# One unit of weights, two batches' products and the copies of own rows assigned to other tiles in the first chunk of a fused mixer and two MLPs

## The chip, the cores and the metric

One core of one Trainium2 chip runs the whole program in a single launch. The metric is device time in microseconds (us), lower is better. Engine names as in the profile: PE is TensorE, PEld its weight loads, DVE is VectorE, ACT is ScalarE, POOL is GpSimd, SP is the queue from which nearly all DMAs are issued.

## The reference, cut to what matters

A state-space mixer over 4 batches of 768 positions, in chunks, then two MLPs on its 3072 tokens of width 256 (hidden width 2048, softplus in the first, a sigmoid gelu in the second):

```python
for c in range(nc):
    cum = np.cumsum(la, axis=-1)
    L = np.exp(cum[:, :, :, None] - cum[:, :, None, :]) * causal
    M = np.einsum('bhin,bhjn->bhij', Cc, Bc) * L
    y_intra = np.einsum('bhij,bhjd->bhid', M, xc)
    y_inter = np.einsum('bhin,bhnd->bhid', Cc, state) * np.exp(cum)[..., None]
    y[:, :, sl] = y_intra + y_inter
    Bx = np.einsum('bhjn,bhjd->bhjnd', Bc, xc) * decay_from_j[:, :, :, None, None]
    state = decay_full[:, :, None, None] * state + np.sum(Bx, axis=2)
...
h = x @ w_in
g = softplus(h)
x = g @ w_out
```

## The kernel before, in words

**Tokens.** The kernel cuts the 768 positions into 6 chunks of 128. A chunk of all four batches is 512 tokens wide. A "batch" number s below counts (chunk, batch) pairs: s = 0 to 3 are chunk 0, s = 4 to 7 chunk 1, and so on up to 23. The mixer of s = 0 to 3 is done ahead of everything; the mixer of s = 4 and up runs spread over the tiles of the first MLP, one chunk ahead of it.

**Tiles.** The first MLP is a loop over t (line 912): 6 chunks of 16 tiles, a tile being 128 of the 2048 hidden columns. `g1` (line 439) makes the tile's hidden values with six matmuls, because both operands are split into a high part that the fast matmul format holds exactly and a low rest (wh·xh, wh·xl, wl·xh for two halves of the contraction). `hidden` is the softplus on ACT. `g2` (line 457) multiplies the tile's activations into the two output accumulators, two tiles later: `g2(t - 2, ...)` is issued at tile t. For the tiles of the first chunk below 10 (`PLAIN`) it is a plain f32 matmul per accumulator on weights `w1of`; from tile 10 on it is three matmuls per accumulator, of which the first reads `w1ol`, the low rest of the output weights, then `w1oh` twice, with `gh` and `gl` (the activation and its rest; `rnd` on ACT, `low` on DVE, a subtraction at line 85).

**Weights.** They arrive as 64-bit words and are put together during the first chunk, in units of 256 columns or rows: `W1_units` lists them, 13 in all, alternately input ("1i") and output ("1o"), and the unit at place u of the list is called unit u here. `unit(t)` (line 895) joins unit t: for an output unit two DVE instructions (lines 148 and 153), for an input unit one (line 161). Where the unit is split, `split` (line 93) puts the copy to the high part (ACT, line 95) and the subtraction that makes the low rest (DVE, line 85, writing `w1il` or `w1ol`) on two lists, which `catch_up` empties in the next tiles. `w_low` does the ACT part of the joining, `w_scale` a scaling on POOL (input, line 130) or ACT (output, line 128). The last units are 9, 11 and 12: the output rows of tiles 10 and 11, 12 and 13, 14 and 15.

**The mixer's steps for one s**, dealt to tiles by hand (k = t mod 4, s = (c + 1)*4 + (t mod 16)//4): `at_scan` (DVE, line 260) makes L; `at_m` (DVE, line 339) multiplies it with the kept product CB, in place, once per half g, giving M; `at_y` and `at_u` (PE, lines 367, 376, 385) make y and the state's increment u for a pair of batches; `at_out` copies y to `xh` on ACT (line 404) and hands back the subtraction for `xl` (DVE, line 85); `at_state` updates the state (DVE, line 419) and calls `at_own` (POOL, line 426), the copy of the state's own rows, which the next `at_y` of that batch reads; `at_small` is `at_bs` (POOL, line 273, reads L, so that `at_m`, which overwrites L, comes behind it) and `at_dc` (DVE line 283, then POOL line 285, giving `cd`). `at_prep` makes masked operands (DVE line 228 twice, then three subtractions on POOL at line 88, writing `lb` and `rhs_bd`) for s = 8 and up. `at_load_a` and `at_load_p` issue DMAs on SP.

**Order.** Everything runs under a manual schedule: each engine, and the SP queue, takes its instructions in the order of the program text. An instruction that waits holds up all that is behind it on its engine. Within a tile of the loop the order is: `at_m`; `w_low`; `low(t - 1)`; `g1`; `g2`; `at_y`/`at_u`; the ACT copies of `at_out`; `hidden`; `rnd`; `catch_up` of the DVE list, then of the ACT list; then by k the block with `xl`, `at_scan`, `at_state`, `at_small`, `at_prep`, the loads; then `unit(t)`.

Before the change, batches 4 and 5 have M at tiles 0, 2, 6 and 7, y and u at tile 7, and `xh`, `xl`, state and `at_small(6)` at tile 8; M of batch 6 is at tiles 9 and 10; the four first `at_own` are at tile 2; unit 12 is joined at tile 12 and its low rest made at tile 14. At tile 15 DVE has `low(14)`, `xl` of batches 6 and 7, the scan of batch 8, the states of 6 and 7.

Of the kernel before, what the change touches and what calls it, by code (L numbers as in the profile page):

```python
# [19 lines left out]
NB, NH, S, D, N = 4, 8, 768, 32, 16  # L20
# [5 lines left out]
NF = DFF // P  # L26
# [17 lines left out]
def mixer_two_mlps(ctx: ExitStack, tc: tile.TileContext, pack_p, pack_q, pack_s, pack_x, a_rows, consts, w1i, w1o, w2i, w2o, out):  # L44
# [46 lines left out]
    act_later, vec_later = [], []  # L91
# [8 lines left out]
    def catch_up(todo):  # L100
        fs = todo[:]
        todo.clear()
        for f in fs:
            f()
# [76 lines left out]
    def at_load(s):  # L181
        at_load_a(s)
        at_load_p(s)
# [14 lines left out]
    def at_load_p(s):  # L198
        c, b = divmod(s, NB)
        d = sub.setdefault(s, {})  # L200
        if c == 0:
            pk = x2[:, (0, 1, 4, 5)[s]].rearrange("p k t -> p (k t)")
            nc.sync.dma_start(out=pk[:, 0:PL_W], in_=pack_p[s])
            d["B"], d["C"], d["x"], d["bn"] = pk[:, 0:PL_C], pk[:, PL_C:PL_X], pk[:, PL_X:PL_BN], pk[:, PL_BN:PL_W]
        else:
            px = at.tile([P, SX_W], F32, tag="px", name=f"px{s}", bufs=3)
            nc.sync.dma_start(out=px, in_=pack_x[s - NB])
            if c > 1:
                pk = at.tile([P, SP_W], F32, tag="pk", name=f"pk{s}")
                nc.sync.dma_start(out=pk, in_=pack_s[s - 2 * NB])  # L210
                d["B"], d["C"] = pk[:, 0:SP_C], pk[:, SP_C:SP_W]
            d["x"], d["bn"], d["ci"] = px[:, 0:SX_BN], px[:, SX_BN:SX_CI], px[:, SX_CI:SX_W]
# [52 lines left out]
    def at_small(s):  # L265
        at_bs(s)
        at_dc(s)
# [60 lines left out]
    def at_m(s, g):  # L328
        d = sub[s]
        l = d["L"][:, 4 * g : 4 * g + 4, :]  # L330
        if s >= NB:
            d["M", g] = l
        elif s == 0:
            d["M", g] = d["cb", g].rearrange("p a t -> p (a t)").rearrange("p (h t) -> p h t", h=4)
        else:
            m = hid.tile([P, TB], F32, tag=("gh", "g", "gh")[s - 1], name=f"M{s}_{g}")
            d["M", g] = m.rearrange("p (h t) -> p h t", h=4)
        m, l = (v.rearrange("p (a h) t -> p a (h t)", a=2) for v in (d["M", g], l))
        (nc.gpsimd if s == 0 else nc.vector).tensor_tensor(out=m, in0=d["cb", g], in1=l, op=ALU.mult)  # L339
# [67 lines left out]
    def at_state(s):  # L407
        c, b = divmod(s, NB)
        d = sub.pop(s)
        if c == NC - 1:  # L410
            return
        u = d["u"]
        st = state[b]
        if s < 2:
            nc.scalar.activation(st, u, AF.Copy)
        elif c == 0:
            nc.vector.tensor_copy(st, u)
        else:
            nc.vector.scalar_tensor_tensor(
                out=st, in0=st, scalar=d["dc"][:, T - 1 : T], in1=u, op0=ALU.mult, op1=ALU.add  # L420
            )
        if c > 0:
            at_own(b)
# [4 lines left out]
    def at_pe(s, k):  # L428
        if k < 2:
            at_cb(s, k)  # L430
        elif k == 2 and s % 2:
            at_y(s - 1, s)
            at_u(s - 1)
            at_u(s)
# [66 lines left out]
    with tc.manual_schedule():  # L501
# [140 lines left out]
        W1_units = []  # L642
        for q in range(6):
            W1_units += [("1i", q + 2), ("1o", q + 1)]
        W1_units += [("1o", 7)]
        SLOT = {7: 0, 8: 1}
        W2_units = [(kind, q) for q in range(8) for kind in ("2i", "2o")]
        W_in = {"1i": w1i, "1o": w1o, "2i": w2i, "2o": w2o}

        def w_low(kind, q):  # L650
            (w_three_sign if kind == "1i" else w_three)(kind, q)
# [243 lines left out]
        def unit(t):  # L895
            nonlocal wt
            kind, q = W1_units[t]
            if kind == "1o":
                w_join_lo(wt, raws[kind, q].bitcast(U32)[:, 0::2])
            if kind == "1o" and 2 * q >= PLAIN:  # L900
                wo_split((w1oh, w1ol), q, w_join_sign(kind, q, wt))
            elif kind == "1o":
                w_join_sign(kind, q, wt, w1of[:, 2 * q : 2 * q + 2, :].rearrange("p m f -> p (m f)"))
            else:
                wi_split(W1, q, w_join(kind, q, wt))
            if t + 1 < len(W1_units):
                wt = w_scale(*W1_units[t + 1], nc.gpsimd if W1_units[t + 1][0] == "1i" else nc.scalar)
            for u in {9: (12,)}.get(t, (t + 5,) if t < 7 else ()):
                kind, q = W1_units[u]
                w_load(W_in[kind], kind, q, SLOT.get(u))  # L910

        for t in range(NT):
            c, m = divmod(t, NF)
            s, k = (c + 1) * NB + m // 4, m % 4
            mixing = c < NC - 1
            ended = (t - 2) // NF if t >= 2 and (t - 2) % NF == NF - 1 else None

            m_at = (2, 3) if s == NB + 1 else (1, 2)
            if mixing and k in m_at and t > 1:
                at_m(s, m_at.index(k))  # L920
            if 1 < t < len(W1_units):
                w_low(*W1_units[t])
            if t > PLAIN:
                low(t - 1)

            if t != 1:
                g1(t, *W1, xh[c], xl[c])
            late = k < 2 or t < NF
            if mixing and not late:
                at_pe(s, k)  # L930
            if t >= 2:
                for j in range(2):
                    g2(t - 2, j)
            if mixing and late:
                at_pe(s, {(NB + 1, 2): 3, (NB + 1, 3): 2}.get((s, k), k))

            pair_done = () if not mixing else (s - 1, s) if k == 3 and s % 2 and s > NB + 1 else (NB, NB + 1) if t == 2 * 4 else ()
            xl_of = [at_out(i) for i in pair_done]
            if t != 1:
                hidden(t)  # L940
            if t >= PLAIN:
                rnd(t)
            if ended is not None:
                finish(ended, 0)
                finish(ended, 1)
            if t == 0:
                g1(1, *W1, xh[c], xl[c])
                hidden(1)
                w_low(*W1_units[0])
                unit(0)  # L950
                at_bs(s)
                at_m(s, 0)
                catch_up(act_later)
                w_low(*W1_units[1])
            catch_up(vec_later)
            catch_up(act_later)

            if t == 2:
                for i in range(NB):
                    at_own(i)  # L960
            if mixing:
                if k == 0 and t > 0:
                    for f in xl_of:
                        f()
                    for i in pair_done:
                        at_state(i)
                    at_small(s)
                elif k == 1:
                    if 2 * NB <= s + 1 < NSUB:
                        at_prep(s + 1)  # L970
                elif k == 3:
                    for f in xl_of:
                        f()
                    if s + 1 < NSUB:
                        at_scan(s + 1)
                    for i in pair_done:
                        at_state(i)
                    if s + 2 < NSUB:
                        at_load(s + 2)
                    if s == NSUB - 1:  # L980
                        at_ctx.close()
                        y_ctx.close()
                        ps_y = ps_ctx.enter_context(tc.tile_pool(name="ps_y2", bufs=2, space=PSUM, reuse_waits="tile"))

            if t == PLAIN - 1:
                w1oh, w1ol = (wts.tile([P, NF, DM], F32R, tag=n, name=n) for n in ("w1oh", "w1ol"))
            if 0 < t < len(W1_units):
                unit(t)
            if t == 1:
                at_dc(s)  # L990
            if NF - 2 <= t < NF - 2 + PLAIN and m % 2 == 0:
                q = (t - NF + 2) // 2
                wo_split((w1oh, w1ol), q, w1of[:, 2 * q : 2 * q + 2, :])
            if t == (NC - 2) * NF:
                for kind, q in W2_units[0:3]:
                    w_load(W_in[kind], kind, q)
                units = [unit_steps(0), unit_steps(1)]
                first, then, srcs = pair_sums(0)
                pair = [first + then]
            if t == (NC - 1) * NF:  # L1000
                second_open()
                pair[0] += pair_split(0, [], srcs)
                units += [unit_steps(u) for u in range(2, 9)]
            if t >= (NC - 1) * NF - 3:
                run(units, pair, "DADAD", True)
# [59 lines left out]
```

## Time and profile before

| | us |
|---|---|
| Median of 3 runs (lowest, highest) | 568.26 (568.26, 568.55) |
| The profiled execution: its own time | 568.49 |
| The profiled execution: span, first to last instruction | 566.7 |
| Busy in the span: PE | 558.0 (98%) |
| Busy in the span: DVE | 441.1 (78%) |
| Busy in the span: ACT | 341.0 (60%) |
| Busy in the span: POOL | 134.2 (24%) |

How to read it: the span is the time between the first and the last instruction; the run's own time is 1.8 us more, for what lies around it. Busy shares are averages over the whole span; what a change of one stage does is read from the timeline of that stage. In the timeline a line has the start, the busy time (of a merged group from its first start to its last end), engine, line, operation, tile names, shapes, a count, and, in brackets, how long the engine had been idle before and what ended that. Matmuls overlap: six of 0.39 us follow one another 0.23 us apart. The first tile's matmuls begin at 21.17 us; tile 7 begins at 39.16, tile 10 at 50.82, tile 14 at 62.91, tile 16 at 71.44.

### The profile page before, as it was taken

Reading aid. Unit: us, or ns where it says so; the run is one execution under the profiler, and the core shown is the slowest. Engines: PE = TensorE matmul, PEld = TensorE weight load, DVE = VectorE, ACT = ScalarE, POOL = GpSimd, SP = SyncE. Lnnn points to the kernel's source line nnn. Section 1 sums busy time; section 2 is a strip of 40 time slices with the busy share of each in tenths; the row PEclk is TensorE's granted clock in tenths of the full one; section 3 lists DMA queues with packets and bytes.
Section 4 is the critical chain, followed back from the end, with each engine's and each line's share of the span. In section 5 each row is a group of like instructions: output and inputs, shape, how many; then the busy total and the mean of one; then the engine's idle time right before and its main releaser. Section 6 shows DMA issues by size and latency. Waiting matters only on the chain.

```text
span 566.7 us, 8296 instructions
## 1 busy us (share of the span) xinstructions
PE 558.0 (98%) x3092; PEld 450.2 (79%) x3092; DVE 441.1 (78%) x645; ACT 341.0 (60%) x574; POOL 134.2 (24%) x128
## 2 busy tenths in 40 slices
PE   8999999999999999999999999999999999999997
PEld 6656788888888888888888788888888888888885
DVE  7999999869787776968888699998976565665754
ACT  4989555444344444435898777867755464654644
POOL 4684474546544544541000000000000000000000
PEclk9999999999999999999999999999999999999999
DMA  8965443341422425211233112000200000200002
GB/s 285 376 195 174 160 134 106 133 154 42 154 90 106 133 104 205 103 56 34 80 110 107 44 41 72 1 1 0 75 1 1 1 1 0 75 0 1 1 1 74
DMA packets 22745, 48.64 MB, mean 86 GB/s; under 512 B 1936, under 2 KB 5168, under 8 KB 22704
## 3 DMA queue, kind: packets, MB, share of 16 engines
q1 hardware_dynamic: 22560, 48.01, 25.5%
q8 instruction: 24, 0.39, 0.3%
q14 instruction: 17, 0.14, 0.1%
q10 hardware_dynamic: 144, 0.10, 0.1%
HBM read 44.76 MB, written 3.34 MB: 85 GB/s over the span
## 4 chain that ended last, share of the span: by engine, by line
PE 86%; DMA 4%; DVE 4%; POOL 2%; ACT 2%; issue 1%; SPq 0%; POOLq 0%; DVEq 0%
PE h L447 20%; PE p L838 19%; PE o L812 8%; PE o L814 8%; PE o L813 8%; PE o L466 7%; PE o L467 6%; PE o L468 6%; DMA wraw_1i<-w1i 2%; PE y L376 2%; DMA px<-pack_x 2%; PE cb L322 1%; PE y L367 1%; POOL so L426 1%; DVE L L260 1%
## 5 line engine op out<-in xcount | busy, mean ns | idle before, releaser
L85 DVE TENSOR_TENSOR gl<-g,gh 128x512 fp32r<-128x512 f32 x182 | 141.1, 777 | 24.4 <-ACT gh L478 23.7
L473 ACT ACTIVATE g<-h 128x512 f32<-128x512 f32 x96 | 57.5, 599 | 107.5 <-PE h L447 95.4
L478 ACT ACTIVATE gh<-g 128x512 fp32r<-128x512 f32 x182 | 115.1, 632 | 5.9
L447 PE MATMUL h<-xh,w1ih 128*128 128x512 f32 x192 | 78.7, 411 | 0.0
L447 PE MATMUL h<-xl,w1ih 128*128 128x512 f32 x192 | 75.1, 392 | 0.0
L844 DVE TENSOR_TENSOR g<-p,x 128x512 f32<-128x512 f32 x72 | 49.6, 689 | 29.6 <-PE p L838 28.2
L466 PE MATMUL o<-gh,w1ol 128*128 128x512 f32 x172 | 68.0, 395 | 0.7 <-DVE w1ol L85 0.7
L467 PE MATMUL o<-gh,w1oh 128*128 128x512 f32 x172 | 67.0, 390 | 0.0
L468 PE MATMUL o<-gl,w1oh 128*128 128x512 f32 x172 | 67.0, 389 | 0.0
L260 DVE TENSOR_TENSOR_SCAN L<-abz,eye 128x1024 f32<-128x1024 f32 (+1 forms) x26 | 63.2, 2439 | 0.7 <-PE abz L250 0.7
L447 PE MATMUL h<-xh,w1il 128*128 128x512 f32 x192 | 59.3, 390 | 0.0
L846 ACT ACTIVATE g<-g 128x512 f32<-128x512 f32 x72 | 45.5, 632 | 20.9 <-DVE g L844 18.5
L88 POOL TENSOR_TENSOR rhs_bd<-tc,pk 64x512 fp32r<-64x512 f32 x32 | 54.8, 1714 | 1.2
L812 PE MATMUL o<-gh,w2ol 128*128 128x512 f32 x120 | 46.8, 390 | 0.4 <-ACT gh L478 0.4
L814 PE MATMUL o<-gl,w2oh 128*128 128x512 f32 x120 | 46.9, 390 | 0.0
L813 PE MATMUL o<-gh,w2oh 128*128 128x512 f32 x120 | 46.7, 389 | 0.0
L846 ACT ACTIVATE g<-p 128x512 f32<-128x512 f32 x24 | 14.3, 594 | 52.4 <-PE p L838 52.3
L447 PEld LDWEIGHTS h<-xh,w1ih 128*128 128x128 f32 x192 | 36.0, 188 | 8.6 <-issue 1.9
L447 PEld LDWEIGHTS h<-xl,w1ih 128*128 128x128 f32 x192 | 36.1, 188 | 8.3 <-issue 2.2
L447 PEld LDWEIGHTS h<-xh,w1il 128*128 128x128 f32 x192 | 36.0, 188 | 7.9
L466 PEld LDWEIGHTS o<-gh,w1ol 128*128 128x128 f32 x172 | 32.3, 188 | 8.6 <-DVE w1ol L85 1.1
L339 DVE TENSOR_TENSOR L<-cb,L 128x512 f32<-128x512 f32 x32 | 21.9, 685 | 20.8 <-PE cb L322 20.4
(193 smaller groups left out, 1057.2 us busy)
## 6 DMA issues: line engine op xcount, KB each, us to landing
abz<-scr_z SPq DMA_DIRECT2D x20, 512.0 KB, 7.1
pk<-pack_s SPq DMA_DIRECT2D x16, 512.0 KB, 4.2
px<-pack_x SPq DMA_DIRECT2D x20, 256.0 KB, 3.4
wraw_2i<-w2i SPq DMA_DIRECT2D x8, 512.0 KB, 4.9
wraw_2o<-w2o SPq DMA_DIRECT2D x8, 512.0 KB, 3.6
out<-ot SPq DMA_DIRECT2D x11, 256.0 KB, 2.0
wraw_1i<-w1i SPq DMA_DIRECT2D x5, 512.0 KB, 5.8
wraw_1o<-w1o SPq DMA_DIRECT2D x5, 512.0 KB, 5.1
```

The costliest lines, as they stand in the source:

```text
L85: nc.vector.tensor_sub(o, x, y)
L260: nc.vector.tensor_tensor_scan(out=d["L"][:, h].rearrange("p h t -> p (h t)"), data0=ab.rearrange("p h t -> p (h t)"), data1=eye8[:, h].re ...
L447: nc.tensor.matmul(h, w[:, k, f], x[:, k, :], start=(n == 0), stop=(n == 5))
L466: nc.tensor.matmul(a, w1ol[:, m, o], d["gh"], start=first, stop=False)
L467: nc.tensor.matmul(a, w1oh[:, m, o], d["gh"], start=False, stop=False)
L468: nc.tensor.matmul(a, w1oh[:, m, o], d["gl"], start=False, stop=last)
L478: nc.scalar.activation(d["gh"], d["g"], AF.Copy)
L812: nc.tensor.matmul(a, wl, d["gh"], start=first, stop=False)
L813: nc.tensor.matmul(a, wh, d["gh"], start=False, stop=False)
L814: nc.tensor.matmul(a, wh, d["gl"], start=False, stop=last)
L838: nc.tensor.matmul(dst, w, x, start=start and i == 0, stop=i == 2, skip_group_check=not start)
L846: nc.scalar.activation(d["g"], src, AF.Gelu_apprx_sigmoid)
```

## The change

It concerns tiles 2 to 15, the first chunk of the first MLP. No instruction is added or taken away; they are placed at other tiles.

- M of batch 5 moves from tiles 6 and 7 to 8 and 9, M of batch 6 from 9 and 10 to 11 and 12 (table `M_AT`); M of batch 7 stays at 13 and 14.
- y and u of batches 4 and 5 move from tile 7 to tile 9; what follows them (`xh`, `xl`, state, `at_small(6)`) moves from tile 8 to tile 10, and the DMA of batch 7's inputs (`at_load_p(7)`) from tile 7 to tile 10.
- The four `at_own` on POOL move from tile 2 to tile 6.
- Unit 12 is joined at the end of tile 14 instead of tile 12, and a new emptying of the DVE list at the very end of tile 15, behind the scan of batch 8 and the states, issues its low rest and that of the first re-split output unit (which stood in tile 16).

```diff
@@ -644,6 +644,7 @@
         SLOT = {7: 0, 8: 1}
+        M_AT = {2: ((4, 1),), 8: ((5, 0),), 9: ((5, 1),), 11: ((6, 0),), 12: ((6, 1),), 13: ((7, 0),), 14: ((7, 1),)}
...
-            m_at = (2, 3) if s == NB + 1 else (1, 2)
-            if mixing and k in m_at and t > 1:
-                at_m(s, m_at.index(k))
+            if t < NF:
+                for i in M_AT.get(t, ()):
+                    at_m(*i)
+            elif mixing and k in (1, 2):
+                at_m(s, k - 1)
...
-            if mixing and late:
-                at_pe(s, {(NB + 1, 2): 3, (NB + 1, 3): 2}.get((s, k), k))
-
-            pair_done = () if not mixing else (s - 1, s) if k == 3 and s % 2 and s > NB + 1 else (NB, NB + 1) if t == 2 * 4 else ()
+            if t == 9:
+                at_pe(NB + 1, 2)
+            elif mixing and late and s != NB + 1:
+                at_pe(s, k)
+
+            pair_done = () if not mixing else (s - 1, s) if k == 3 and s % 2 and s > NB + 1 else (NB, NB + 1) if t == 10 else ()
...
-            if t == 2:
+            if t == 6:
                 for i in range(NB):
                     at_own(i)
             if mixing:
-                if k == 0 and t > 0:
+                if t == 10:
                     for f in xl_of:
                         f()
                     for i in pair_done:
                         at_state(i)
+                    at_small(s)
+                    at_load_p(s + 1)
+                elif k == 0 and t not in (0, 8):
                     at_small(s)
...
                     if s + 2 < NSUB:
-                        at_load(s + 2)
+                        (at_load_a if t == 7 else at_load)(s + 2)
...
-            if 0 < t < len(W1_units):
+            if 0 < t < len(W1_units) - 1:
                 unit(t)
+            if t == NF - 2:
+                unit(len(W1_units) - 1)
+            if t == NF - 1:
+                catch_up(vec_later)
```

## Rows read from the trace of the kernel before

**Rows 1.** Waits of PE, whole span: us in total, times, longest.

```profile
PE o L466 <- DVE w1ol L85: 0.7, 1, 0.7
```

**Rows 2.** Timeline of PE, tiles 7 to 16: start, busy, what, [idle before].

```profile
43.38 1.35 PE L376 MATMUL y<-L,px 128*32 128x128 f32 x32
...
50.82 0.79 PE L447 MATMUL h<-xh,w1ih 128*128 128x512 f32 x1
...
65.12 0.50 PE L466 MATMUL o<-gh,w1ol 128*128 128x512 f32 x1 [0.69 <-DVE w1ol L85]
...
67.33 1.08 PE L376 MATMUL y<-L,px 128*32 128x128 f32 x32
...
68.56 0.50 PE L447 MATMUL h<-xh,w1ih 128*128 128x512 f32 x1
...
72.80 0.39 PE L466 MATMUL o<-gh,w1ol 128*128 128x512 f32 x1
```

**Rows 3.** Windows: busy us (count) of PE, PEld, DVE, ACT, POOL, then clock, DMA.

```profile
44.88:64.43 19.55, 19.55 (x76) 13.09 (x70) 18.85 (x29) 16.39 (x27) 5.26 (x7) 1.00 0.60 201
```

**Rows 4.** Timeline of DVE, tiles 7 to 14.

```profile
43.10 1.15 DVE L339 TENSOR_TENSOR L<-x,L 128x512 f32<-128x512 f32 x1
44.17 2.28 DVE L260 TENSOR_TENSOR_SCAN L<-abz,eye 128x1024 f32<-128x1024 f32 x1
...
48.27 0.75 DVE L85 TENSOR_TENSOR xl<-y,xh 128x256 fp32r<-128x256 f32 x2
...
50.94 0.93 DVE L339 TENSOR_TENSOR L<-cb_0k,L 128x512 f32<-128x512 f32 x1 [0.56 <-POOL bs L273]
...
53.57 0.68 DVE L339 TENSOR_TENSOR L<-cb_1k,L 128x512 f32<-128x512 f32 x1
54.17 0.68 DVE L85 TENSOR_TENSOR w1il<-wt_1i,w1ih 128x512 fp32r<-128x512 f32 x1
...
55.38 0.68 DVE L85 TENSOR_TENSOR gl<-g,gh 128x512 fp32r<-128x512 f32 x1
...
61.73 0.66 DVE L148 SCALAR_TENSOR_TENSOR wt_1o<-wt_1o,wraw_1o 128x512 uint32<-128x512 uint32 x1
...
63.19 0.68 DVE L339 TENSOR_TENSOR L<-x,L 128x512 f32<-128x512 f32 x1
...
64.39 0.68 DVE L85 TENSOR_TENSOR w1ol<-wt_1o,w1oh 128x512 fp32r<-128x512 f32 x1
```

**Rows 5.** Timeline of POOL, tiles 2 to 16.

```profile
32.17 4.42 POOL L426 TENSOR_TENSOR so<-st,cc 128x64 f32<-128x64 f32 x4
...
49.38 1.15 POOL L426 TENSOR_TENSOR so<-st,cc 128x64 f32<-128x64 f32 x2 [4.81 <-DVE st L419]
...
59.10 0.62 POOL L273 TENSOR_TENSOR bs<-px,L 128x128 f32<-128x128 f32 x1 [5.84 <-PE h L447]
...
65.55 3.87 POOL L88 TENSOR_TENSOR lb<-tb,pk 128x512 fp32r<-128x512 f32 x1 [2.83 <-DVE tb L228]
69.38 1.29 POOL L88 TENSOR_TENSOR rhs_bd<-tc,pk 64x512 fp32r<-64x512 f32 x1
...
70.74 3.16 POOL L88 TENSOR_TENSOR rhs_bd<-tc,pk 64x512 fp32r<-64x512 f32 x1
```

**Rows 6.** The page's DMA issues: count, KB each, median us from issue to landing.

```profile
px<-pack_x SPq DMA_DIRECT2D x20, 256.0 KB, 3.4
```

**Rows 7.** Timeline of DVE, tile 15 to tile 18.

```profile
69.39 0.76 DVE L85 TENSOR_TENSOR xl<-y,xh 128x256 fp32r<-128x256 f32 x2 [1.12 <-ACT xh L404]
70.06 2.75 DVE L260 TENSOR_TENSOR_SCAN L<-abz,eye 128x1024 f32<-128x1024 f32 x1
72.74 0.44 DVE L419 SCALAR_TENSOR_TENSOR st<-st,dc,y 128x64 f32<-128x64 f32 x2
73.11 1.35 DVE L85 TENSOR_TENSOR gl<-g,gh 128x512 fp32r<-128x512 f32 x1
...
80.44 1.77 DVE L85 TENSOR_TENSOR w1ol<-x,w1oh 128x512 fp32r<-128x512 f32 x1
```

## The prediction

> **What bounds the kernel now.** I read four views, in this order. The busy table of the page says PE is busy for 558.0 of 566.7 us, so no move of work on other engines can gain more than the few us in which PE stands still; and of those only the ones inside tiles 2 to 15 are in reach. The waits of PE name just one there: the accumulator's matmul with `w1ol`, 0.7 us, once [rows 1]. PE's timeline places it at 65.12 us, the first matmul of g2(12) in tile 14, idle for 0.69 us, and that first matmul then takes 0.50 us where one that follows without a gap takes 0.39 [rows 2]: it should have started at 64.43 and costs 0.69 + 0.11 = 0.80 us. The timeline also shows a smaller loss that the list of waits doesn't: the intra-chunk matmuls of y of batches 4 and 5 take 1.35 us, those of batches 6 and 7, the same 32 matmuls, 1.08 [rows 2]. The 0.27 us between them stand beside M of batch 5 on DVE, issued at 43.10 and done only at 44.25 [rows 4]. So the stage holds 0.80 + 0.27 = 1.07 us that could be had, 0.19% of the time. The windows say why DVE is the late one: from the end of that y to the point where PE stops, DVE is busy for 18.85 of 19.55 us, while PE has no idle time at all and the granted clock is 1.00 [rows 3]. PE sets the pace, DVE follows it with a backlog, and shows through where the backlog meets a due time. After tile 16 no wait of PE of this kind is listed, so a loss there is paid in full, and so is a gain.
>
> **The change part by part.** It adds and removes no instruction, so the sum is made of waits alone.
>
> *y of batches 4 and 5 to tile 9.* Its M is then due 2 tiles (some 6 us) later, while M moves by 2 tiles in a queue that already ran behind PE; DVE, relieved of it in tiles 6 and 7, reaches it ahead of the due time. Gain 0.27 us; at worst 0. PE arrives at tiles 8 and 9 some 2 us earlier, because y no longer stands in front of them; what they need (weights of unit 4, activations) is made before y in the order of DVE and ACT, old and new, so I cost this at nothing.
>
> *The four copies of own rows to tile 6.* They held POOL for 4.42 us from 32.17 [rows 5]; POOL's scaling for unit 4 comes earlier now. y needs the copies at tile 9. DVE wins a little slack, PE nothing, since it has no wait there. Cost 0.
>
> *What follows y, to tile 10.* ACT's copies, xl, the states, then POOL's copies and bs, then M of batch 6, which now waits behind bs at tile 11. DVE queues behind that wait: this is the term that decides whether g2(12) is on time. By rows: y must end 0.27 us earlier than tile 10 began, at 50.55. xl starts 69.39 - 68.56 = 0.83 behind the end of y [rows 2, 7], M 50.94 - 48.27 = 2.67 behind xl [rows 4], so M of batch 6 starts at 54.05. From the second M of batch 6 to the end of unit 11's low rest DVE took 65.07 - 53.57 = 11.50 us; of that the new order has already done the two instructions between 54.17 and 55.38 (1.21), no longer has the two joins of unit 12 from 61.73 to 63.19 (1.46), and has one M more (0.93, as at 50.94) [rows 4]: 9.76. The low rest of unit 11 is ready at 63.81. PE asks for it at 64.43 - 0.27 = 64.16. So it comes 0.35 us early, and the 0.80 us are gained whole. Between the bounds it is 0.80 or, with the margin used up, less: see the last rival.
>
> *The DMA of batch 7's inputs, from tile 7 to 10.* On SP it now stands behind the load of unit 12 and waits for y's end (50.55); with the median 3.4 us [rows 6] it lands at about 54, and its first reader, bs of batch 7, ran at 59.10 [rows 5]. Loads of batch 8 queue behind it on SP and are used at tile 13, three tiles later. Cost 0.
>
> *Unit 12 to tile 14, its low rest to the end of tile 15.* The joins fall before low(14), in the place that M and the low rest had there; that is covered, since DVE stood idle for 1.12 us before xl of tile 15 [rows 7]. The low rest isn't covered. It is now behind xl, the scan of batch 8 and the states, and g2(14), the second group of matmuls in tile 16, begins with `w1ol` of that unit. In the old trace the end of y of batches 6 and 7 is at 68.56 and g2(14) starts at 72.80, 4.24 us later, with PE working all the way [rows 2]. From that same end DVE has xl at 69.39, the scan at 70.06, the states at 72.74, and its next place starts at 73.11, already 0.31 us too late; what stood in it, low(15), is a subtraction of the same shape and took 1.35 us, to 74.46 [rows 7]. The low rest of unit 12 now has that place. The chain hangs on the end of y, so it moves with PE. Stall: 74.46 - 72.80 = 1.66 us, and 0.11 for the first matmul after a gap: 1.77. Bounds: the same subtraction took 0.68 at 64.39, the scan 2.28 at 44.17 instead of 2.75 [rows 4, 7], which leaves 1.66 - 0.67 - 0.47 = 0.52, with the restart 0.63; and one of `w1ol` took 1.77 at 80.44 [rows 7], which makes 2.08, with the restart 2.19. I take 1.77, because the row is from the very place. low(15) follows two subtractions later, but is due one tile behind; nothing.
>
> *Why that place is slow.* The scan and low(15) run beside POOL's subtractions for batch 8: the first `rhs_bd` ends at 70.67 and the scan stretches, the second starts at 70.74 and takes 3.16, to 73.90, and low(15) ends 0.56 after it [rows 5, 7]. They take turns. The Trainium skill (SBUF — State Buffer, Who interferes with whom) says that a DVE instruction with two SBUF inputs and a GpSimd instruction that reads SBUF hold a shared port as an exclusive lock, and whoever issues first has it for the whole instruction. These rows agree with it. `lb`, issued at 65.55, took 3.87 us [rows 5], although the DVE instructions issued after it kept their pace; this row speaks against the second half of that rule.
>
> **The sum.** -0.27 - 0.80 + 1.77 = +0.70 us. Against the profiled execution's own time of 568.49 that is 569.19; that execution lies 0.23 above the median of the runs, so against the median of 568.26 it is **568.96, say 569.0 us**, +0.12%. About 0.2% (1.14 us) is what a measurement of this kernel can tell from no change, so the forecast is "no change", with the stall moved from tile 14 to tile 16.
>
> **The rivals.**
>
> *The stall at tile 16 is short.* If POOL's `lb` and `rhs_bd` get through earlier, the scan and the low rest run alone. For it: the masked operands are ready earlier against y's end, since the low rest of unit 11 is, and unit 12's joins are another kind of instruction, between which `lb` may get in. Against it: `lb` was held up until DVE went idle [rows 5]. Then the cost is 0.63 at the lower bound: -1.07 + 0.63 = -0.44, 567.8 us; halfway, 1.2, it is 568.4. By the rule just cited `lb` would go first and lead here.
>
> *No stall at tile 16*: -1.07 us, 567.2. This would need the scan's chain to be 0.3 us shorter than any row allows, and the subtraction free. Everything in [rows 7] speaks against it.
>
> *Slower: g2(12) stays late as well.* M of batch 6 stands behind bs, and bs behind the two copies of own rows on POOL, which took 1.15 us at 49.38, but 1.1 us each when DVE was at a scan, at 32.17 [rows 5]. If they take the latter, M starts 2 x 1.1 - 1.15 = 1.05 later; it decides from 0.35 on. The stall at tile 14 is then 1.05 - 0.35 = 0.70 and the gain there nothing: -0.27 + 1.77 = +1.50, 569.8 us, slower by 0.26%. Against it: while these copies run, DVE has only a short scan and unit 10's join, and then idles.
>
> **How the numbers follow.** Chances: the forecast 0.54, the short stall 0.27, no stall 0.06, late at both places 0.13. The forecast's own range by its bounds is 568.4 to 569.4 (+0.1 to +1.12). The range of 8 in 10 takes in most of the short stall, and of the slower rival all but its far end: 567.7 to 569.7. Faster by over 0.2% would need all of the 1.07 us and a little luck in the measurement: 0.04. Slower by over 0.2%: the slower rival and the forecast's upper edge, 0.15. Within: 0.81.
>
> **What would show it.** Right: no wait of PE for `w1ol` at tile 14; y of batches 4 and 5 with 1.08 us for its 32 matmuls; a new wait of PE for `w1ol`, about 1.7 us, in tile 16, ended by a DVE subtraction that follows the states directly. Wrong in size if that subtraction takes 0.7 us or the scan 2.3; wrong in kind if PE has no idle time in tile 16, or if the wait at tile 14 is still there.

## The result, and the profile after

The changed kernel takes **571.88 us** (median of 6 runs, 571.17 to 573.09) where the kernel before takes 568.44 (6 runs, 568.26 to 568.59): a ratio of **1.0062, 95% interval 1.0052 to 1.0072**. It is slower by 3.4 us, and outside the predicted range.

The profiled execution of the changed kernel has a span of 570.7 us, 4.0 more than before. PE's waits, whole span (us in total, times, longest), those of tiles 14 to 16:

```profile
PE o L466 <- DVE w1ol L85: 1.9, 2, 1.7
PE h L447 <- DVE xl L85: 1.2, 1, 1.2
```

The first was there before, with 0.7 once [rows 1]; the second is new and no part of the forecast. PE's timeline places them:

```profile
49.60 1.08 PE L376 MATMUL y<-L,px 128*32 128x128 f32 x32
...
50.84 0.50 PE L447 MATMUL h<-xh,w1ih 128*128 128x512 f32 x1
...
53.65 0.79 PE L447 MATMUL h<-xh,w1ih 128*128 128x512 f32 x1
...
64.33 0.50 PE L466 MATMUL o<-gh,w1ol 128*128 128x512 f32 x1 [0.18 <-DVE w1ol L85]
...
67.77 0.50 PE L447 MATMUL h<-xh,w1ih 128*128 128x512 f32 x1
...
70.63 0.39 PE L447 MATMUL h<-xh,w1ih 128*128 128x512 f32 x1
72.20 0.50 PE L447 MATMUL h<-xl,w1ih 128*128 128x512 f32 x1 [1.19 <-DVE xl L85]
...
75.37 0.79 PE L466 MATMUL o<-gh,w1ol 128*128 128x512 f32 x1 [1.74 <-DVE w1ol L85]
75.96 0.63 PE L467 MATMUL o<-gh,w1oh 128*128 128x512 f32 x1
76.39 0.63 PE L468 MATMUL o<-gl,w1oh 128*128 128x512 f32 x1
```

Read against [rows 2], in order. The 32 matmuls of y of batches 4 and 5 take 1.08 us instead of 1.35: gained, as forecast. g2(12) waits 0.18 instead of 0.69. Up to the start of tile 16 (70.63, before 71.44) PE is 0.81 us ahead, of the 1.07 that were forecast. Then its second matmul, the first that reads `xl`, waits 1.19 us; g2(14) waits 1.74 and starts at 75.37, 2.57 later than before (72.80). And the matmuls behind it follow at 0.43 us instead of 0.23: the rest of the 4.0 us.

That last part is the clock. Windows of the changed kernel (busy us and count of PE, PEld, DVE, ACT, POOL, then granted clock, DMA share, GB/s):

```profile
68.00:71.00 3.00, 3.00 (x13) 2.13 (x12) 2.96 (x4) 1.88 (x5) 1.60 (x1) 1.00 0.63 137
71.00:72.20 1.20, 0.01 (x1) 0.00 (x0) 1.20 (x4) 1.06 (x2) 0.00 (x0) 1.00 0.75 294
72.20:73.60 1.40, 1.40 (x5) 0.86 (x5) 1.40 (x1) 0.00 (x0) 0.00 (x0) 1.00 0.05 18
73.60:75.37 1.77, 0.03 (x2) 0.01 (x1) 1.77 (x5) 1.23 (x2) 0.36 (x1) 0.86 0.06 9
75.37:78.09 2.72, 2.72 (x6) 2.14 (x7) 1.91 (x3) 0.00 (x0) 2.08 (x4) 0.50 0.57 190
```

PE stood still in the two waits, 1.2 and 1.7 us with 1.4 of work between them; in the second the granted clock falls, and the six matmuls of g2(14) run at 0.50, which is the 1.2 GHz level. This is not in every execution: three runs (571.17, 571.23, 571.24) have a mean clock of 0.999 to 1.000, three (572.52, 572.70, 573.09) of 0.996 to 0.997. So the two waits cost some 2.8 us net, and the clock 1.3 to 1.9 more in half of the runs.

Why are `xl` and the low rest late? DVE's timeline of tiles 10, 11 and 13 to 16, and POOL's:

```profile
51.66 0.76 DVE L85 TENSOR_TENSOR xl<-y,xh 128x256 fp32r<-128x256 f32 x2 [1.17 <-ACT xh L404]
...
54.34 0.94 DVE L339 TENSOR_TENSOR L<-cb_0k,L 128x512 f32<-128x512 f32 x1 [0.56 <-POOL bs L273]
...
62.73 0.94 DVE L85 TENSOR_TENSOR gl<-g,gh 128x512 fp32r<-128x512 f32 x1
63.60 0.68 DVE L85 TENSOR_TENSOR w1ol<-wt_1o,w1oh 128x512 fp32r<-128x512 f32 x1
...
64.99 1.78 DVE L339 TENSOR_TENSOR L<-x,L 128x512 f32<-128x512 f32 x1
66.69 1.76 DVE L85 TENSOR_TENSOR gl<-g,gh 128x512 fp32r<-128x512 f32 x1
68.38 1.77 DVE L148 SCALAR_TENSOR_TENSOR wt_1o<-wt_1o,wraw_1o 128x512 uint32<-128x512 uint32 x1
70.19 0.69 DVE L153 SCALAR_TENSOR_TENSOR wt_1o<-wraw_1o,wt_1o 128x512 uint32<-128x512 uint32 x1
70.80 0.69 DVE L85 TENSOR_TENSOR gl<-g,gh 128x512 fp32r<-128x512 f32 x1
71.40 0.75 DVE L85 TENSOR_TENSOR xl<-y,xh 128x256 fp32r<-128x256 f32 x2
72.06 2.28 DVE L260 TENSOR_TENSOR_SCAN L<-abz,eye 128x1024 f32<-128x1024 f32 x1
74.26 0.45 DVE L419 SCALAR_TENSOR_TENSOR st<-st,dc,y 128x64 f32<-128x64 f32 x2
74.63 0.68 DVE L85 TENSOR_TENSOR w1ol<-wt_1o,w1oh 128x512 fp32r<-128x512 f32 x1
```

```profile
62.31 0.82 POOL L285 TENSOR_TENSOR cd<-dc,px 128x128 f32<-128x128 f32 x1 [2.77 <-DVE dc L283]
64.75 1.47 POOL L88 TENSOR_TENSOR lb<-tb,pk 128x512 fp32r<-128x512 f32 x1 [1.63 <-DVE tb L228]
66.18 1.72 POOL L88 TENSOR_TENSOR rhs_bd<-tc,pk 64x512 fp32r<-64x512 f32 x1
...
67.98 1.62 POOL L88 TENSOR_TENSOR rhs_bd<-tc,pk 64x512 fp32r<-64x512 f32 x1
```

Before, `lb` took 3.87 us [rows 5] and the DVE instructions beside it kept 0.68. Now `lb` takes 1.47, and M, low(13) and the first join of unit 12 take 1.78, 1.76 and 1.77: each of the three ends about 0.6 us after one of POOL's three subtractions does, so each spends some 1.1 of its 1.8 us waiting. DVE comes to `xl` 3.63 us after the end of y instead of 0.83 (67.77 to 71.40), and the scan, the states and the low rest all follow that. The scan and the low rest themselves now run undisturbed (2.28 and 0.68).

### The profile page after: what moved, and what is told of

It is laid out like the page before. It is cut to its first block, busy times and chain, and to the rows that moved or that the text cites. A ratio compares the mean times of both kernels' runs of the same rounds, so it can differ in the third digit from the quotient of the medians.

```text
span 570.7 us, 8292 instructions
## 1 busy us (share of the span) xinstructions
PE 560.7 (98%) x3092; PEld 451.9 (79%) x3092; DVE 443.3 (78%) x645; ACT 340.8 (60%) x574; POOL 130.3 (23%) x128
## 4 chain that ended last, share of the span: by engine, by line
PE 91%; DVE 4%; ACT 2%; issue 1%; POOL 1%; DMA 0%; DVEq 0%; POOLq 0%
PE h L447 21%; PE p L839 19%; PE o L815 8%; PE o L813 8%; PE o L814 8%; PE o L466 7%; PE o L467 6%; PE o L468 6%; PE o L464 2%; PE y L376 2%; PE cb L322 1%; PE abz L250 1%; PE y L367 1%; DVE gl L85 1%; PE cb L296 1%
```

## The experiments

**1. Without POOL's three subtractions for batch 8.** `lb` is copied on ACT and `rhs_bd` left at zero for this batch: PE still runs batch 8's product, but it comes out as zero.

```diff
+        if s == 2 * NB:
+            nc.scalar.activation(d["lb"].rearrange("p a t -> p (a t)"), tb.bitcast(F32), AF.Copy)
+            return
         psub(d["lb"].rearrange("p a t -> p (a t)"), tb.bitcast(F32), d["B"])
```

> The changed kernel without POOL's three subtractions for batch 8 (lb is copied on ACT, rhs_bd left at zero for this batch, so batch 8's product is not computed). Theory, the port: in the changed kernel the M, low(13) and first join of tile 14 take 1.78, 1.76 and 1.77 us because each waits for one of these subtractions; without them each takes about 0.7, xl of batches 6 and 7 starts at the end of y + 0.8, PE's wait for xl (1.19 us) is gone, the wait for unit 12's low rest shrinks to about 0.5, the granted clock stays at 1.00, and the time is 568.0 to 568.4. Rival, the queue: DVE simply has too many instructions ahead of xl in tiles 14 and 15; then the three keep well over 1 us or xl is still late by over 0.5 us, and the time stays above 570.

568.47 us, ratio to before 1.0002 (0.9993 to 1.0010). DVE's timeline (lines shifted by three):

```profile
64.96 0.68 DVE L342 TENSOR_TENSOR L<-x,L 128x512 f32<-128x512 f32 x1
65.56 0.68 DVE L85 TENSOR_TENSOR gl<-g,gh 128x512 fp32r<-128x512 f32 x1
66.17 0.68 DVE L148 SCALAR_TENSOR_TENSOR wt_1o<-wt_1o,wraw_1o 128x512 uint32<-128x512 uint32 x1
...
68.56 0.76 DVE L85 TENSOR_TENSOR xl<-y,xh 128x256 fp32r<-128x256 f32 x2 [0.39 <-ACT xh L407]
```

The three take 0.68, `xl` waits for ACT and not for DVE, the wait of PE for it is gone, and that for the low rest is 0.43. The 3.4 us come from POOL's subtractions (571.88 - 568.47). The queue alone, the rival, is not it: without them DVE even stands idle for 0.39 us ahead of `xl`. The time is 0.07 above what was expected.

**2. Unit 12 back at tile 12**, the other moves kept.

```diff
-            if 0 < t < len(W1_units) - 1:
+            if 0 < t < len(W1_units):
                 unit(t)
-            if t == NF - 2:
-                unit(len(W1_units) - 1)
-            if t == NF - 1:
-                catch_up(vec_later)
```

> The changed kernel with unit 12 joined at tile 12 again and its low rest at tile 14, the other moves kept. Theory, the port and the late low rest: the wait at tile 14 comes back larger (1.3 to 1.7 us, since M of batch 6 is late and the two joins are in front again), no wait for unit 12's low rest in tile 16. If POOL's subtractions take turns with DVE in tile 14 as in the changed kernel, PE still waits 0.3 to 0.7 us for xl: 569.3 to 569.9; if POOL is held up as in the kernel before: 568.9 to 569.3. Rival, that the moved products and copies are the harm and not unit 12: 571 or more.

569.09 us, 1.0013 (1.0004 to 1.0021). PE waits 1.38 us at tile 14 and not at all in tile 16; POOL is held up exactly as before (`lb` 3.87). So the other moves alone cost 0.7 us. M of batch 6 waits 0.56 us for POOL's bs, no more than before. What is new stands ahead of it: DVE is idle for 1.16 us in tile 10, because y has only just ended, and unit 11's low rest is ready at 65.49, 0.42 us later than before, where PE comes 0.27 earlier.

**3. Unit 12 alone moved**, in the kernel before (the same lines the other way round).

> The kernel before with unit 12 alone moved. Theory: the wait at tile 14 is gone (-0.80), y of batches 4 and 5 keeps its 1.35 us. If the move of unit 12 is enough to let POOL take turns with DVE in tile 14, the waits for xl and for unit 12's low rest are there as in the changed kernel, and the time is 571 to 573; if POOL is held up as before, only the wait for the low rest of about 1.7 us is there, and it is 569.0 to 569.5.

570.94 us, 1.0052 (1.0036 to 1.0067): `lb` 1.47, M, low(13) and the join 1.78, 1.76 and 1.78, waits of PE of 0.99 for `xl` and 1.72 for the low rest. Moving unit 12 alone brings both new waits, and about 2.5 of the 3.4 us.

**4. The low rest ahead of the scan** in tile 15.

```diff
                     for f in xl_of:
                         f()
+                    if t == NF - 1:
+                        vec_later.pop(0)()
```

> The changed kernel with unit 12's low rest put ahead of the scan of batch 8 in tile 15. Theory: the wait of PE for xl at tile 16 stays (about 1.2 us), the wait for unit 12's low rest (1.74) is gone, the granted clock doesn't fall, so about 1.85 us under the faster runs of the changed kernel: 569.1 to 569.6. Rival, that the second wait follows from the first alone and not from the place of the low rest: still a wait over 1 us there, time above 570.5.

569.99 us, 1.0027 (1.0017 to 1.0038). The wait for the low rest is gone (0.17 is left, at tile 14), that for `xl` is 1.16, the clock stays at 0.999 or 1.000 in all seven runs. The second wait comes from the place of the low rest. The time is 0.4 above the range given: with the scan later, M of batch 8 is late and PE waits 0.38 us for it at the next product.

**5. and 6. Is it how long POOL had been idle?** In the changed kernel `lb` starts after 1.63 us of idle POOL, before after 2.83; against M its start is 0.24 us ahead in both. Run 5 makes batch 7's `cd` earlier in the changed kernel, run 6 gives POOL work just ahead of `lb` in the kernel before.

```diff
             if t < NF:
+                if t == 12:
+                    at_dc(s)
                 for i in M_AT.get(t, ()):
...
-                    at_small(s)
+                    (at_bs if t == 12 else at_small)(s)
```

> The changed kernel with batch 7's scan of decays ahead of the second M of batch 6 in tile 12, so that POOL's cd is done some 2 us earlier and POOL is idle for about 3 us before lb of batch 8, as in the kernel before (2.83) and unlike the changed one (1.63). Theory A (how long POOL stood idle decides whether lb gets in at once): lb is held up until DVE has a gap, about 3.9 us; M, low(13) and the join take 0.7 each; xl is on time; the wait for unit 12's low rest of about 1.7 us is left: 568.9 to 569.4. Theory B (the place of lb against M decides, which doesn't change): lb takes about 1.5, the three DVE instructions about 1.77 each, 571 or more.

```diff
+        if s == 2 * NB:
+            nc.gpsimd.tensor_tensor(out=touch, in0=w1ol[:, 13, 0:16].bitcast(F32), in1=own[:, 0:16], op=ALU.mult)
         psub(d["lb"].rearrange("p a t -> p (a t)"), tb.bitcast(F32), d["B"])
```

> The kernel before with one small POOL product (128 x 16, into a tile that nobody reads) that waits for the low rest of unit 11, so that POOL is busy just ahead of lb of batch 8. Theory A: lb now takes about 1.5 us instead of 3.87, the M, low(13) and low rest of tile 14 take about 1.77 each, xl comes late, PE waits 0.3 to 0.8 us for it, 568.7 to 569.3 (g2(14) has its weights in time here). Theory B: lb still takes 3.5 us or more and the time is that of the kernel before.

Run 5: 570.55 us, 1.0049 (1.0035 to 1.0062), and neither theory's numbers. M goes ahead of `lb`, as A said, but `lb` isn't held up to the gap. POOL's and DVE's timelines:

```profile
64.71 3.26 POOL L88 TENSOR_TENSOR lb<-tb,pk 128x512 fp32r<-128x512 f32 x1 [2.83 <-DVE tb L228]
```

```profile
65.55 0.68 DVE L85 TENSOR_TENSOR gl<-g,gh 128x512 fp32r<-128x512 f32 x1
66.15 0.68 DVE L148 SCALAR_TENSOR_TENSOR wt_1o<-wt_1o,wraw_1o 128x512 uint32<-128x512 uint32 x1
66.86 1.65 DVE L153 SCALAR_TENSOR_TENSOR wt_1o<-wraw_1o,wt_1o 128x512 uint32<-128x512 uint32 x1
68.44 1.77 DVE L85 TENSOR_TENSOR gl<-g,gh 128x512 fp32r<-128x512 f32 x1
```

Most instructions here start 0.60 us after the one before and take 0.68, so they overlap. The second join reads what the first writes and starts 0.71 after it, when that has ended; `lb` gets in there. The second join and low(14) wait, the scan takes 2.71, and PE waits 2.15 us for the low rest. Run 6: 568.25, 0.9999 (0.9990 to 1.0008), `lb` 3.86: against A.

**7. `lb` issued behind M**: the two masks of batch 8 in the other order.

```diff
-        for o, i, mask in ((tb, d["B"], mB), (tc_, d["C"], mC)):
+        for o, i, mask in ((tb, d["B"], mB), (tc_, d["C"], mC))[:: -1 if s == 2 * NB else 1]:
```

> The changed kernel with the two masks of batch 8 in the other order, so that lb (which reads the one now second) is issued about 0.15 us behind M instead of 0.24 ahead of it. Theory B (who is first keeps the port through a run of DVE instructions without a gap): M goes first, lb is held up to the first gap, the DVE instructions keep 0.7 us, only the wait for the low rest of about 1.7 us is left: 568.9 to 569.4. Theory A: lb gets in behind M, low(13) and both joins or the join take 1.77, xl is as late as in the changed kernel, 571 or more.

571.06 us, 1.0052 (1.0038 to 1.0066). `lb`, issued 0.16 us behind M, is held up past M, low(13) and the first join, and gets in between the two joins as in run 5 (second join 1.66, low(14) 1.77, PE's wait 2.18). Two of the four runs are at full clock, 570.34 and 570.36. B was right that M then keeps POOL out, but not for how long.

**8. A version from what was found.** Batch 8's masked operands are one scaled copy each on ACT, which reads nothing that DVE or POOL writes, and unit 12's high part is copied at the end of tile 14, so that its low rest falls ahead of `xl`.

```diff
+        if s == 2 * NB:
+            d["lb"] = at.tile([P, 4, T], F32R, tag="lb", name=f"lb{s}", bufs=1)
+            nc.scalar.activation(d["lb"].rearrange("p a t -> p (a t)"), d["B"], AF.Copy, scale=nB)
+            for j in range(2):
+                q = slice(64 * j, 64 * j + 64)
+                nc.scalar.activation(rhs_bd[q, :, j, :], d["C"][q].rearrange("p (a t) -> p a t", a=4), AF.Copy, scale=nC[q])
+            return
...
             if t == NF - 2:
                 unit(len(W1_units) - 1)
-            if t == NF - 1:
-                catch_up(vec_later)
+                catch_up(act_later)
```

`nB` and `nC` are the masks less one, two more columns of the constants.

> The changed kernel with batch 8's masked operands made on ACT by one scaled copy each (no masks on DVE, no subtractions on POOL for this batch), and unit 12's high part copied at the end of tile 14, so that its low rest comes ahead of xl in tile 15. Theory: nothing holds up DVE in tiles 14 and 15, xl and the low rest are both in time, the only waits left are those that both kernels have and at most 0.2 us at tile 14: 567.3 to 567.7, under both kernels. Rival, that the moves themselves cost something else: above 568.2.

567.63 us, **0.9989 (0.9980 to 0.9998)**: faster than the kernel before by its interval, and than the changed one by some 4 us. Of the waits in tiles 14 to 16 only one is left:

```profile
64.41 0.50 PE L474 MATMUL o<-gh,w1ol 128*128 128x512 f32 x1 [0.18 <-DVE w1ol L86]
```

**9. and 10. The two joins apart**, the first ahead of low(13), the second behind it, so that no neighbour needs the other's result: run 9 on run 5, run 10 on the changed kernel.

```diff
+            if t == NF - 2:
+                w_join_lo(wt, raws["1o", 7].bitcast(U32)[:, 0::2])
             if t > PLAIN:
                 low(t - 1)
...
-            if kind == "1o":
+            if kind == "1o" and q < 7:
                 w_join_lo(wt, raws[kind, q].bitcast(U32)[:, 0::2])
```

> The kernel with batch 7's scan of decays early (there lb was held up until between the two joins of unit 12), with these two joins no longer next to each other: the first ahead of low(13), the second behind it. The second needs the first's result, so DVE can't start it while the first still runs; every other pair in this run overlaps. Theory C (POOL gets the port only where DVE leaves such a gap): lb is now held up to the gap ahead of xl, about 3.9 us, M, low(13) and both joins take 0.7 each, xl starts at the end of y + 0.8, only the wait for the low rest of 1.6 to 1.9 us is left, 568.9 to 569.5. Rival D (after some time POOL gets in between any two instructions): lb still ends about 3.3 us after its start, one join or low(14) takes over 1.6, the wait is 2.1 or more, above 570.

> The changed kernel with the two joins of unit 12 apart in the same way. There lb was ahead of M. Theory C: M waits for lb (1.78), then POOL finds no gap and the first rhs_bd is held up to the gap ahead of xl; xl is at most 0.5 us late for its own start and in time for PE; a wait for the low rest of 1.6 to 2.2 us is left: 568.9 to 569.7. Rival D: the three subtractions each hold up one DVE instruction as in the changed kernel, xl late by over 2 us, 571 or more.

Run 9: 571.67 us, 1.0055 (1.0042 to 1.0069), its one run with the clock at 1.000 at 570.44. POOL's and DVE's timelines:

```profile
65.02 4.48 POOL L88 TENSOR_TENSOR lb<-tb,pk 128x512 fp32r<-128x512 f32 x1 [2.83 <-DVE tb L228]
```

```profile
67.06 0.68 DVE L153 SCALAR_TENSOR_TENSOR wt_1o<-wraw_1o,wt_1o 128x512 uint32<-128x512 uint32 x1
67.67 0.68 DVE L85 TENSOR_TENSOR gl<-g,gh 128x512 fp32r<-128x512 f32 x1
68.87 0.76 DVE L85 TENSOR_TENSOR xl<-y,xh 128x256 fp32r<-128x256 f32 x2 [0.52 <-ACT xh L404]
69.54 3.35 DVE L260 TENSOR_TENSOR_SCAN L<-abz,eye 128x1024 f32<-128x1024 f32 x1
72.82 0.44 DVE L419 SCALAR_TENSOR_TENSOR st<-st,dc,y 128x64 f32<-128x64 f32 x2
73.19 1.32 DVE L85 TENSOR_TENSOR w1ol<-wt_1o,w1oh 128x512 fp32r<-128x512 f32 x1
```

With the joins apart `lb` is held up to the gap ahead of `xl`, and nothing else in tile 14 waits: theory C's mechanism. Its time was wrong: the scan takes 3.35, because the first `rhs_bd` begins just ahead of it, and PE waits 2.15 us, not 1.6 to 1.9. Run 10: 572.10 us, 1.0058 (1.0042 to 1.0074): M 1.78, the first join 1.76, low(13) 1.78, the second join 0.68. PE waits 0.32 us for low(13), 0.44 for `xl` and 1.74 for the low rest; the two runs at full clock take 571.00 and 571.09. There POOL needs no gap, and rival D of this run is right: once `lb` is ahead, its successors take turns with DVE even where DVE's instructions overlap.

**11. The ACT operands in the kernel before**, the moves left out (the first part of run 8's edit).

> The kernel before with batch 8's masked operands made on ACT. Theory: the two waits of the kernel before (0.7 us at tile 14, 0.27 in y of batches 4 and 5) stay, since both lie ahead of this work, so 568.1 to 568.5; the gain of the combined version over the kernel before then belongs to the moves. Rival, that the gain comes from taking the work off POOL and DVE alone: 567.8 or less.

568.41 us, 1.0001 (0.9993 to 1.0010). The wait of 0.72 at tile 14 stays. The operands on ACT bring nothing by themselves; they make room for the moves. Nor do they account for all of run 8: experiment 1, which also has the moves without POOL's subtractions but leaves the low rest behind the scan, waits 0.43 us for it and stands at 568.47. That the rest of the gain comes from the earlier low rest wasn't tried by itself.

**12. POOL's idle time once more**, in the kernel before.

```diff
+            if t == 13:
+                nc.gpsimd.memset(x2[:, 1, 0, 0:16], 0.0)
```

> The kernel before with one small POOL memset (128 x 16, over values already used) that waits for the first M of batch 7, so that POOL's last work ends about 1.5 us before lb of batch 8, as in the changed kernel (1.63), instead of 2.83. Everything DVE does is unchanged. Theory A (POOL's idle time before lb decides whether it is ahead of M): lb takes about 1.5 us, M, low(13) and the low rest in tile 14 about 1.77 each, PE waits 0.3 to 0.9 us for xl; 568.7 to 569.4. Rival E (it is decided on DVE's side, by how long ago DVE last had to wait for POOL): lb is held up for 3.87 us and the time is that of the kernel before.

568.43 us, 1.0001 (0.9992 to 1.0011): POOL idle for 1.51 us ahead of `lb`, and `lb` still 3.87. Theory A falls for good. E agrees with all runs that have `lb` start 0.23 or 0.24 us ahead of M, but wasn't tried by itself: where `lb` goes first (the changed kernel, runs 3, 4 and 10), the last DVE instruction held up by POOL ended 1.1 us before `lb` (low(12), 62.73 + 0.94, and 64.75); in the kernel before and in runs 2, 5, 6, 9 and 12 it ended 2.3 us before. What makes the order is left open.

## Why the prediction was wrong

*What bounds the kernel, and the two old losses.* Right: the 0.27 us of y came back whole. The term of g2(12) was mis-sized: 0.80 was forecast with 0.35 us in hand, the wait is still 0.18. Its chain was right step by step (`xl` 0.82 us behind the end of y, M 2.68 behind `xl`, as forecast), but unit 11's low rest is ready at 64.28 and not at 63.81. Of these 0.47 us 0.29 stand at the chain's start: y ended at 50.84, not 50.55, because the first matmul of a tile behind y takes 0.50 where one behind a plain g2 takes 0.79, so that y's gain is seen at tile 11 (53.65, before 53.92) and not yet at tile 10. The other 0.18 is low(12), which meets `cd` of batch 7 and takes 0.94, 0.26 more than counted, less 0.08 elsewhere.

*"The joins fall before low(14) ... that is covered."* This step failed. It put the joins where M and the low rest had stood, though M of batch 7 stays at tile 14; only the low rest leaves. That slip did no harm: experiment 1 shows that at the old pace the joins are covered. What failed is the pace. The step took it that DVE's instructions there would keep 0.68 us because they did before. That rested on POOL being held up for 3.87 us [rows 5], which belonged to that order of instructions and not to `lb`. With unit 12 moved, POOL's subtractions got in, DVE lost 3.3 us ahead of `xl`, and PE met a wait that no case had. Experiments 1 and 3 show it. Why `lb` gets in at its start there and not before is open (experiment 12).

The other pace could be read before the change. Thirteen us later in the kernel before, `lb` of the next batch takes 1.41 us, and POOL and DVE then alternate. DVE's subtraction at 80.44 took its 1.77 us there [rows 7]; the prediction used that row only as an upper bound for one subtraction. The lines around it:

```profile
78.56 1.41 POOL L88 TENSOR_TENSOR lb<-tb,pk 128x512 fp32r<-128x512 f32 x1 [2.33 <-issue]
79.93 1.74 POOL L88 TENSOR_TENSOR rhs_bd<-tc,pk 64x512 fp32r<-64x512 f32 x1
81.74 1.62 POOL L88 TENSOR_TENSOR rhs_bd<-tc,pk 64x512 fp32r<-64x512 f32 x1
```

```profile
79.34 1.18 DVE L85 TENSOR_TENSOR gl<-g,gh 128x512 fp32r<-128x512 f32 x1
...
82.14 1.78 DVE L85 TENSOR_TENSOR gl<-g,gh 128x512 fp32r<-128x512 f32 x1
```

*The short-stall rival had the event and not its price.* It said that `lb` might get in, and by the cited rule would; it then let the scan and the low rest run alone, which they did, and forgot that whoever lets POOL in waits: the 1.1 us that POOL takes is paid by a DVE instruction, and if that stands ahead of `xl` instead of behind it, it costs more. So a case that is slower stood in the forecast as a faster one. "No stall" never came near.

*The stall at tile 16.* Its place was right and its cause, the low rest behind scan and states, too: experiment 4 removes it. Its size of 1.66 us agrees with the measured 1.74 by luck, since that stands on a late `xl` and an undisturbed scan: by the forecast's own signs the scan of 2.28 and the subtraction of 0.68 meant a far shorter stall. (The forecast's own range begins at 568.4, the halfway stall of 1.2, and not at its lower bound of 0.63; nothing that came hangs on that.) Where M goes ahead of `lb` and nothing is let in ahead of `xl`, the run nearest to the forecast's own case, it is 2.15 (experiment 9), above the forecast's upper bound without restart of 2.08: the bound took the scan at 2.75, and there it takes 3.35, beside a first `rhs_bd` that begins 0.07 us ahead of it and not 0.68.

*The slower rival* (late at both places) named POOL's two copies of own rows as its cause, and they took 1.15 us as before. Late at tile 14 by 1.38 us is only experiment 2, with unit 12 left in place.

*What no part had:* the clock. After the two waits it was down in half of the runs. Two waits may not be needed for that: in experiments 5, 7 and 9 the long wait (2.15 to 2.18 us) is the only one in tile 16, and 1, 2 and 3 of their four runs have a mean clock of 0.996 or 0.997 (none of these runs has a trace, so where it fell isn't shown). In experiment 4, whose longest wait in the stage is 1.16, none of seven has. The stall that was forecast may thus have had a price beyond its own length.

## What to carry to other kernels

A DVE duration read beside POOL work holds only for that order of instructions: before moving anything there, ask for each instruction which of the two waits if it goes the other way, and whether the loser stands ahead of a due time. A dependent pair can be a gap: where an instruction started after the end of the one before instead of 0.08 us before it, POOL got in (experiments 5 and 7), and with the pair apart it didn't (experiment 9). Look for the other pace elsewhere in the trace before trusting one row. Work that holds up DVE only because it was put on POOL can go to ACT where that has time, which then lets the rest move (experiment 8).

## What the runs showed of the hardware

Two ways of sharing, in one place of one program. A POOL subtraction of 128x512 was held up by a run of overlapping DVE instructions for 3.87 us in the kernel before, 4.48 with one more of them (experiment 9), and got in only where DVE paused, for 0.03 us between two dependent joins (experiments 5 and 7) or longer; in each of these cases it ended 1.14 or 1.15 us after the DVE instruction ahead of the pause. The same subtraction ahead of the same M ended after 1.47 us, and its two successors then alternated with DVE at 1.1 us of wait each, with no pause of DVE. The Trainium skill (SBUF — State Buffer, Who interferes with whom) states that issue order decides who blocks. The changed kernel and run 10 agree with it (`lb` 0.24 and 0.23 us ahead of M, M 1.78); the kernel before and runs 2, 5, 6, 9 and 12 don't, with the same lead of 0.23 or 0.24 us, and M at 0.68. So issue order as the trace shows it isn't enough to tell who goes first.
